# An attention and MLP kernel: the planner's order of operations replaced by a stored table, with other planner settings and full-width products for the first values

## The chip, the cores and the metric

The kernel runs on one core of a Trainium2 chip. A core has a matrix engine (TensorE, PE in the profile, with its weight loads as PEld), a vector engine (VectorE, DVE), a scalar engine (ScalarE, ACT), a general engine (GpSimd, POOL), a queue engine that here only issues DMAs (SyncE, SP), the on-chip memory, and PSUM, eight banks of 128 partitions by 512 float32 that receive the matrix products. Each engine works through its own list of instructions in order, and waits where an instruction needs something that another engine has not finished. The metric is the device time of one execution in microseconds.

## The reference

One input `x` of 2048 rows and 640 columns (bfloat16) goes through two branches, which a gate mixes row by row:

```
g = sigmoid((x * gate_w).sum(-1))
a = softmax(q k^T / sqrt(20)) v, 32 heads of 20 columns, then @ wo       # q, k, v from x @ wqkv
h = x @ w1 + b1 ;  act = h * tanh(softplus(h)) ;  b = act @ w2           # 640 -> 1536 -> 640
out = g * a + (1 - g) * b
```

The attention has 32 heads of 2048 by 2048 scores, all of which pass through an exponential. They are most of the work.

## The kernel before

**Units.** The 32 heads are taken in eight quads `p` of four heads (one head for each 32-row strip of the matrix engine), and the 2048 query columns in four chunks `c` of 512. A pair (p, c) is a group; there are 32 groups of 64 units. A unit is one product of scores: 128 keys of one head by 512 queries, which fills one PSUM bank. Four units that follow one another use the four strips and run beside each other. This is written "S" below: an S operation holds one to four score products.

**Exponentials.** A unit's bank is emptied in one of two ways. ScalarE takes two neighbouring banks (sometimes three or one) through `Exp` into the buffer `E` of 34 slots (line 1122). Or VectorE writes a straight-line approximation of the exponential as 16-bit integers (`psum_chord`, line 1154), and two more versions of it with another offset are made from that copy, each for two units at once, by GpSimd or by VectorE (`line`, line 1172; queue `xq`). A chord unit then enters the next product three times instead of once.

**Values.** The product of `E` with the values is made for four heads at once, in the four 32-column strips ("P", one to four products, into the accumulator bank 7). Two chunks of `VA`, the values with a column of ones, come from `add_v`: j = 0 are the 80 columns of the first four heads, which every unit of the first quad needs.

**The rest of the matrix work** are `Misc` operations: transposes of `x` (`xt`), the projections of queries and keys (`k0`, `q0` for the first quad, blocks `kb`, `qb` for the others), the values (`v0`, `v1`, `v2`), the first and second products of the MLP (`h`, `w2`) and the output projection (`wo`). Each takes a bank, some pieces of matrix work, and one evacuation, mostly by VectorE. Query and key blocks are stored to DRAM and loaded back into strips of the right partitions (`add_blk`, `add_strips`); queries of the first quad's chunks 1 to 3 take this way too, chunk 0 does not.

**Matrix engine modes.** Score products use 32 rows by 128 columns of the array (mode "R"), value products and projections 128 rows by 32 columns, four at a time (`mm4`, mode "C"), transposes the whole array (mode "T").

**What sets the order.** `make_plan` plays the kernel through on the host, with a clock and a duration for every operation. Whenever an engine is free in this play, a function (`poll_pe`, `poll_act`, `poll_dve`, `poll_gp`, `poll_sp`) chooses its next operation from what is ready, by due times and by the numbers in `PAR`, of which those ending in `_2` hold from unit 1700 of 2048 on. What it chooses is appended to `pl.out`, and the kernel is emitted in just that order:

```
    plan = make_plan(K, PAR)
    for fn in plan["pl"].out:
        fn()
```

On the chip only each engine's own order and the data matter; waits are put in wherever an operation touches bytes that an earlier one wrote or read. The settings that the change touches: `v0` moves the due time of the first values (`add_v(0, t, 2 * t - par["v0"])`, due counted in pairs of units, beside `xt` at -100 + 2i, `k0` at -92 + 8c, the first query blocks from -25.6 on); `slack` is how long after the planned end of an exponential its value product may be planned; `elow` is the count of free `E` slots at or under which value products go ahead of projections; `hold` and `idlek` bear on score operations of fewer than three units; `xmin`, `xwait`, `gpmax` and `xb` divide the offset copies between GpSimd and VectorE; `last` keeps the last units from the chord; `wl`, `wp`, `wo` are due times of MLP and output products; `mgb` delays the planned release of a bank.

Of the kernel before, what the change touches and what calls it, by code (L numbers as in the profile page):

```python
# [11 lines left out]
P = 128  # L12
# [8 lines left out]
KT, FT, NS = 5, 12, 16  # L21
# [31 lines left out]
for _c in range(NQC):  # L53
# [8 lines left out]
    "dvw": 38.53743660585776,  # L62
    "gpmax": 3438.021927551807,
    "xmin": 2062.5527122350004,
    "xwait": 349.421302746659,
    "urgent": 22.640125992529832,
    "kq": 2.9970653505716234,
    "v0": 80.0,
    "slack": 154.76747254069397,
    "fill": 0.64,  # L70
    "h0": 3.5649434246577676,
    "h1": 16.826758018508038,
    "w0": 10.794573911905426,
    "w1": 23.39035664805156,
    "hl": 6.335275894690732,
    "wl": 5.8531955315483435,
    "last": 5.05082387060483,
    "mb": 9,
    "elow": 12.382529619172656,
    "ahd": 6.0,  # L80
    "age": 6.220859528764049,
    "eres": 0.014480172002720943,
    "vk": 3,
    "a3": 4,
    "a3gp": 1688.8815596232141,
    "hold": 5,
    "idlek": 5,
    "swait": 155.25662470383708,
    "flush": 8,
    "tailh": 0,  # L90
    "dahead": 387.7453029112783,
    "mgb": 0.0,
    "xb": 0.0,
    "ph": 1700.6915314751984,
    "wp": 30.113523199568974,
    "wo": 26.20880268482808,
    "thr_2": 317.7585558513145,
    "lead_2": 123.43702968058237,
    "gpmax_2": 4098.35985412354,
    "xmin_2": 2880.9153602384567,  # L100
    "xwait_2": 537.2401013960538,
    "vk_2": 3.0,
    "a3gp_2": 1925.808193077294,
    "dahead_2": 447.85548472553995,
    "age_2": 9.211581861796914,
    "ahd_2": 3.0816465538756317,
    "hold_2": 4.0,
    "idlek_2": 3.0,
    "mb_2": 7.0,
    "dvw_2": 36.65964931310165,  # L110
    "slack_2": 253.79751934331,
    "mgb_2": 0.0,
    "xb_2": 1.0,
}

# [5 lines left out]
XAT = [3900.0, 5300.0, 8500.0, 10500.0, 12700.0]  # L121


class Names:
    pass


class Misc:
    def __init__(self, name, due, need, pieces, evac, dur, gives):
        self.name, self.due, self.need = name, due, need  # L130
        self.pieces, self.evac, self.dur, self.gives = pieces, evac, dur, gives
        self.bank = None
        self.i = 0


class Clock:
# [4 lines left out]
    def __init__(self):  # L141
        self.t = 0.0
        self.ev = []
        self.n = 0
        self.free = {e: 0.0 for e in self.LAT}
        self.tok = set()
        self.busy = {e: 0.0 for e in self.LAT}
        self.log = []
        self.out = []
        self.ops, self.cur, self.pend, self.res, self.prov = [], (), [], {}, {}  # L150

    def at(self, t, fn, cur=None):
# [18 lines left out]
    def src(self, toks):  # L171
        return tuple(i for x in toks for i in self.prov.get(x, ()))

    def run(self, eng, occ, done=None, lat=None, rd=(), wr=(), dep=(), kind=""):
        i = len(self.ops)
        deps = set(dep) | set(self.pend)
        self.pend = []
        for r in rd:
            v = self.res.setdefault(r, [None, []])
            deps.add(v[0])  # L180
        for r in wr:
            v = self.res.setdefault(r, [None, []])
            deps.add(v[0])
            deps.update(v[1])
        deps.discard(None)
        for r in rd:
            self.res[r][1].append(i)
        for r in wr:
            self.res[r] = [i, []]
        if lat is None:  # L190
            lat = occ + (36.0 if eng == "GP" else 90.0 if eng in ("DVE", "ACT") else 0.0)
        self.free[eng] = self.t + occ
        self.busy[eng] += occ
        self.log.append((eng, self.t, occ))
        self.ops.append((eng, occ, lat, deps, kind, self.t))
        self.at(self.free[eng], lambda: None)
        if done is not None:
            self.at(self.t + lat + self.LAT[eng], done, (i,))
# [44 lines left out]
def make_plan(K, par):  # L243

    pl = Clock()
# [78 lines left out]
    def bank(b):  # L324
        return K.ps[:, b, :]

    def mm(o, l, r, first, last, pos):
        K.nc.tensor.matmul(o, lhsT=l, rhs=r, start=first, stop=last, tile_position=pos, skip_group_check=True)  # L328

    def mm4(o, l, r, first, last, cols=P):  # L330
        for q in range((cols + 31) // 32):
            w = min(32, cols - 32 * q)
            mm(o[32 * q : 32 * q + w, :], l[:, 32 * q : 32 * q + w], r, first, last, (0, 32 * q))
# [87 lines left out]
    def add_v(j, t0, due):  # L421
        c0, w, h0, nh, nt = VR[j]

        def pc(i, kt, b):
            t = t0 + i
            o = bank(b)[:, i * w : (i + 1) * w]
            mm4(o, K.xT[:, kt, t * P : (t + 1) * P], K.wv[:, kt, c0 : c0 + w], kt == 0, kt == KT - 1)

        def ev(b):
            src = bank(b)[:, 0 : nt * w].rearrange("p (t c) -> p t c", t=nt)  # L430
            o = 1 if j == 1 else 0
            for i in range(nt) if nt != 1 else [0]:
                K.nc.vector.tensor_copy(
                    out=K.VA[:, t0 + i, h0 * VS : (h0 + nh) * VS].rearrange("p (h d) -> p h d", d=VS)[:, :, 0:DH],
                    in_=src[:, i, o : o + nh * DH].rearrange("p (h d) -> p h d", d=DH),
                )
            if j == 1:
                K.nc.vector.tensor_copy(out=K.zt[:, t0 : t0 + nt], in_=src[:, :, 0])

        pieces = []  # L440
        for i in range(nt):
            for kt in range(KT):
                pieces.append((max(w / 2.4, 50.0) + 2.0, "C", (lambda b, i=i, kt=kt: pc(i, kt, b)), ()))
        gives = [("v", j, t0 + i) for i in range(nt)] + ([("z", t0 + i) for i in range(nt)] if j == 1 else [])
        dur = nt * (75 + nh * DH / 0.96) + (70 if j == 1 else 0)
        need = [("xT", t0 + i) for i in range(nt)] + ["wv0" if j == 0 else "wv"]
        misc.append(Misc(f"v{j}.{t0}", due, need, pieces, ev, dur, gives))
# [169 lines left out]
    for c in range(NQC):  # L617
        for f in range(FT):
            k = c * FT + f
# [4 lines left out]
    for t in range(NS):  # L624
        for half in range(2):
            k = 2 * t + half
# [60 lines left out]
    def late_par(k):  # L687
        return par[k + "_2"] if nxt[0] >= par["ph"] else par[k]
# [6 lines left out]
    mode = [None]  # L695
# [5 lines left out]
        return nxt[0] / 2  # L701

    def pe_run(md, dur, done=None, **kw):
        sw = 0.0 if mode[0] == md else 111.0
        mode[0] = md
        recent.append((pl.t + sw, dur))
        pl.run("PE", dur + sw, done, **kw)

    def misc_lim():
        return (NBANK if opn["out"] else NBANK - 2) if opn["tail"] else 3 if opn["lent"] else int(late_par("mb"))  # L710
# [453 lines left out]
    def gp_backlog():  # L1164
        return sum(q[0] for q in gp_q) + 1125.0 * len(xq) + max(0.0, pl.free["GP"] - pl.t)

    xq, lock = [], [0.0]
# [6 lines left out]
    def run_x():  # L1174
        if not xq:
            return False
        idle = pl.free["GP"] <= pl.t and lock[0] <= pl.t and len(xq) >= 2 and not gp_q and late_par("xb") >= 1
        if not idle and (gp_backlog() < late_par("xmin") or lock[0] > pl.t + late_par("xwait")):
            return False
        e0, e, k, w, fin = xq.pop(0)  # L1180
        emit(lambda: line(K.nc.vector, e0, e, k, w))
        wait = max(0.0, lock[0] - pl.t)
        d = 337.0 if w == 2 else 197.0
        lock[0] = pl.t + wait + d - 47.0
        stat["x"] += 1
        pl.run("DVE", wait + d, fin, rd=[("E", e0 + i) for i in range(w)], wr=[("E", e + i) for i in range(w)], kind="X%d" % w)
        return True

    def poll_dve():
# [42 lines left out]
        if run_x():  # L1232
            return True
# [42 lines left out]
        def done():  # L1276
            freed(b)
            push(x, n, h, 0)
            if h == 1:
                third(x, 2)  # L1280
# [16 lines left out]
    def third(x, w):  # L1297
        done = set()

        def fin(k):  # L1300
            done.add(k)
            if len(done) == 2:
                read.add(x[0][0])
                for q in [q for q in held if held[q] == x[0][0]]:
                    del held[q]
                    efree.add(q)
            for n, h in x[2]:
                push(x, n, h, k, len(done) == 2)

        for k in (1, 2):  # L1310
            xq.append((x[0][0], x[0][k], k, w, lambda k=k: fin(k)))

    def flush():
        x, half[0] = half[0], None
# [4 lines left out]
    def poll_gp():  # L1319
        wait = max(0.0, lock[0] - pl.t)  # L1320
        if gp_q:
            dur, fn, done = gp_q.pop(0)
            emit(fn)
            lock[0] = pl.t + wait + dur - 80.0
            pl.run("GP", wait + dur, done, kind="G")
            return True
        if xq:
            e0, e, k, w, fin = xq.pop(0)
            emit(lambda: line(K.nc.gpsimd, e0, e, k, w))
            d = 1125.0 if w == 2 else 650.0  # L1330
            lock[0] = pl.t + wait + d - 82.0
            pl.run("GP", wait + d, fin, rd=[("E", e0 + i) for i in range(w)], wr=[("E", e + i) for i in range(w)], kind="L%d" % w)
            return True
        return False
# [126 lines left out]
def kernel(  # L1461
# [14 lines left out]
    K = Names()  # L1476
# [98 lines left out]
    nc.gpsimd.memset(K.ont, 0.0)  # L1575

    plan = make_plan(K, PAR)
    for fn in plan["pl"].out:
        fn()


# [28 lines left out]
```

## Time and profile before

| | us |
|---|---|
| executions shown | 747.53, 747.78, 748.13 (median 747.78) |
| the profiled execution | 748.59 |
| its span, first to last instruction | 746.7 |

| engine | busy us | share of the span | instructions |
|---|---|---|---|
| PE, matrix products | 731.5 | 98% | 10514 |
| ACT | 715.9 | 96% | 753 |
| DVE | 601.5 | 81% | 1049 |
| POOL | 500.5 | 67% | 466 |

A busy time is the union of an engine's instructions. Matrix products overlap, and their ends are modelled, so that the share of PE says little of how dense the work is: a product of 512 columns is shown 383 ns long, where the next set of four can start after some 217 ns. In the same way an exponential of 1024 columns is shown 1103 ns long, and the next one starts 904 ns after it. Distances from start to start are therefore the better measure for both.

### The profile page before, as it was taken

What the parts mean: (1) busy time and instruction counts of PE and PEld (TensorE: products, weight loads), DVE (VectorE), ACT (ScalarE), POOL (GpSimd) and SP (SyncE); (2) the same over time, 40 slices, a digit from 0 to 9 for tenths busy, and PEclk for the clock granted to TensorE, in tenths of its full rate; (3) what the DMA queues carried; (4) which work ended last, traced back from release to release, by engine and by line L of the source; (5) the groups of instructions that cost most, each with busy time, mean ns of one, the idle gap of its engine ahead of it and who ended that gap; (6) DMA issues with size and microseconds to landing.
All of it is one profiled execution on the core that took longest, in us unless ns stands there. A gap on an engine that the chain in (4) does not pass through costs nothing.

```text
span 746.7 us, 25298 instructions
## 1 busy us (share of the span) xinstructions
PE 731.5 (98%) x10514; PEld 249.9 (33%) x10514; DVE 601.5 (81%) x1049; ACT 715.9 (96%) x753; POOL 500.5 (67%) x466
## 2 busy tenths in 40 slices
PE   8899999999999999999999999999999999999997
PEld 4443322222224433333332222223433333323333
DVE  4478888888888988779888888888998888878785
ACT  6869999999999999999999999999999999999995
POOL 9126666766666767757566755766866678688884
PEclk9999999999999999999999999999999999999999
DMA  9611301020011111112111110003411101212212
GB/s 286 213 61 47 89 17 28 24 61 21 22 28 39 33 30 30 49 41 83 30 44 30 48 45 16 28 22 92 134 48 30 30 25 52 80 51 63 68 38 69
DMA packets 45723, 41.87 MB, mean 56 GB/s; under 512 B 20120, under 2 KB 39240, under 8 KB 45608
## 3 DMA queue, kind: packets, MB, share of 16 engines
q1 hardware_dynamic: 42984, 39.94, 18.0%
q8 instruction: 82, 1.34, 0.8%
q10 hardware_dynamic: 2624, 0.31, 0.3%
q14 instruction: 33, 0.27, 0.1%
HBM read 27.59 MB, written 12.38 MB: 54 GB/s over the span
## 4 chain that ended last, share of the span: by engine, by line
PE 80%; ACT 11%; DVE 4%; issue 3%; DMA 1%; POOL 1%; SPq 0%; POOLq 0%; DVEq 0%; ACTq 0%
PE ps L328 79%; ACT E L1122 11%; DVE E L1154 2%; DVE E L1172 1%; DMA rd_d<-rden 0%; PE ps L1558 0%; POOL E L1172 0%; DMA rb<-rd_d 0%; DVE accs L1213 0%; POOL ost L1031 0%; ACT xT L346 0%; POOL R L1425 0%; PE ps L338 0%; SPq L1411 0%; DVE ost L506 0%
## 5 line engine op out<-in xcount | busy, mean ns | idle before, releaser
L1122 ACT ACTIVATE E<-ps 128x1024 bf16<-128x1024 f32 (+1 forms) x726 | 682.8, 1121 | 19.5 <-PE ps L328 18.6
L1172 POOL TENSOR_SCALAR E<-E 128x1024 uint16<-128x1024 uint16 x396 | 436.6, 1103 | 231.4 <-DVE E L1154 187.0
L1154 DVE TENSOR_SCALAR E<-ps 128x512 uint16<-128x512 f32 x567 | 380.6, 685 | 102.4 <-PE ps L328 92.3
L328 PE MATMUL ps<-qT,kT 32*128 32x512 bf16 x2048 | 287.9, 383 | 4.4 <-ACT E L1122 2.4
L328 PE MATMUL ps<-E,VA 128*32 128x512 bf16 x3182 | 288.8, 383 | 1.1 <-DVE E L1154 0.4
L328 PEld LDWEIGHTS <-kT 32*128 32x128 bf16 x2048 | 78.0, 90 | 271.5 <-issue 266.9
L328 PEld LDWEIGHTS <-VA 128*32 128x32 bf16 x3182 | 72.1, 95 | 93.5 <-issue 81.8
L1172 DVE TENSOR_SCALAR E<-E 128x1024 uint16<-128x1024 uint16 x172 | 95.6, 556 | 7.8 <-DVE E L1154 0.5
L328 PE MATMUL ps<-R,act 128*32 128x320 bf16 x1536 | 84.3, 302 | 0.4 <-DVE E L1154 0.2
L328 PE MATMUL ps<-xT,R 128*32 128x512 bf16 x960 | 79.7, 383 | 0.3 <-ACT E L1122 0.2
L328 PEld LDWEIGHTS <-R 128*32 128x32 bf16 (+1 forms) x1728 | 38.9, 95 | 44.9 <-issue 37.4
L328 PEld LDWEIGHTS <-act 128*32 128x32 bf16 x1536 | 35.5, 95 | 33.9 <-issue 26.1
L328 PE MATMUL ps<-wk,R 128*32 128x320 bf16 (+1 forms) x640 | 39.6, 303 | 0.4 <-ACT E L1122 0.3
L328 PE MATMUL ps<-wv,xT 128*32 128x80 bf16 (+2 forms) x960 | 36.6, 257 | 1.6 <-issue 1.6
L454 DVE TENSOR_SCALAR act<-ps,b1f 128x512 bf16<-128x512 f32 x48 | 35.4, 738 | 1.1 <-PE ps L328 0.7
L328 PE MATMUL ps<-xT,wk 128*32 128x512 bf16 (+1 forms) x360 | 33.2, 383 | 0.0
L1425 POOL TENSOR_TENSOR ons<-accs,rb 128x512 bf16<-128x512 f32 x24 | 31.0, 1293 | 2.6 <-DMA rb<-rd_d 1.1
L328 PE MATMUL ps<-xT,wq 128*32 128x512 bf16 x400 | 32.1, 382 | 0.0
L385 DVE CAST stg<-ps 128x512 bf16<-128x512 f32 (+1 forms) x40 | 27.3, 682 | 2.4 <-PE ps L328 2.3
L328 PEld LDWEIGHTS <-xT 128*32 128x32 bf16 x960 | 19.6, 96 | 15.2 <-issue 10.9
L1213 DVE COPY accs<-ps 128x512 f32<-128x512 f32 x31 | 21.2, 683 | 2.7 <-PE ps L328 2.3
L1046 ACT ACTIVATE act<-act 128x3072 bf16<-128x3072 bf16 x8 | 21.5, 2752 | 0.0
(72 smaller groups left out, 190.1 us busy)
## 6 DMA issues: line engine op xcount, KB each, us to landing
rb<-rd_d SPq DMA_DIRECT2D x124, 64.0 KB
qd<-stg SPq DMA_DIRECT2D x20, 128.0 KB
b_d<-bst SPq DMA_DIRECT2D x16, 160.0 KB
out_dram<-ost SPq DMA_DIRECT2D x16, 160.0 KB
kT<-kd SPq DMA_DIRECT2D x28, 80.0 KB
qT<-qd SPq DMA_DIRECT2D x28, 80.0 KB
stg<-b_d SPq DMA_DIRECT2D x13, 160.0 KB
kd<-stg SPq DMA_DIRECT2D x16, 128.0 KB
```

Of the source, the lines that this page charges most:

```text
L328: K.nc.tensor.matmul(o, lhsT=l, rhs=r, start=first, stop=last, tile_position=pos, skip_group_check=True)
L385: K.nc.vector.tensor_copy(out=K.stg[0:w, s, :], in_=bank(b)[0:w, :])
L454: K.nc.vector.tensor_scalar(out=K.act[:, f, (c % 2) * QC : (c % 2 + 1) * QC], in0=bank(b), scalar1=K.b1f[:, f : f + 1], scalar2=None, op0= ...
L1046: K.nc.scalar.activation(a, a, ACT.Mish)
L1122: lambda: K.nc.scalar.activation(K.E[:, e : e + w, :], K.ps[:, b0 : b0 + w, :], ACT.Exp, scale=SCALE)
L1154: lambda: K.nc.vector.tensor_scalar(out=K.E[:, e + h, :].bitcast(U16), in0=K.ps[:, b, :], scalar1=CH_MUL, scalar2=CH_OFF + CH_ADD[0], op0= ...
L1172: eng.tensor_scalar(out=o, in0=i, scalar1=float(CH_ADD[k]), scalar2=1.0, op0=ALU.add, op1=ALU.mult)
L1213: emit(lambda: K.nc.vector.tensor_copy(out=K.accs[:, g % 2, :], in_=K.ps[:, ACCB, :]))
L1425: gp_q.append((1350.0, lambda: K.nc.gpsimd.tensor_tensor(out=dst(), in0=K.accs[:, b, :], in1=K.rb[:, b, :], op=ALU.mult), lambda: pl.give( ...
```

## The change

- Twenty-two numbers of `PAR` are others, among them `v0` 80 to 64.3, `elow` 12.4 to 20.2, `hold` 5 to 6, `xb` 0 to 1, `slack` 154.8 to 142.0 and `slack_2` 253.8 to 154.4, `gpmax_2` 4098 to 5779, `xmin_2` 2881 to 3533, `mgb_2` 0 to 18.8.
- The pieces of the first values (j = 0) are one product with 128 weight columns each, in mode T, instead of four with 32 in mode C. The host's play counts 62 instead of 50 for such a piece.
- In the host's play, a change of mode costs less where PE has been idle, and GpSimd takes an offset copy at the earliest 90 ns after it was queued.
- Each operation of the plan keeps the emitting functions that belong to it (`fns`), and the kernel emits the operations in the order of a table, `ORDER`, instead of the plan's own. Three hexadecimal digits stand for each operation: its number in the plan, counted from the lowest one not yet emitted. The table has 5,411 entries. Operations that touch the same bytes stay in sequence.

```
-    "slack": 154.76747254069397,
+    "v0": 64.32986463352033,
+    "slack": 141.97275980676932,
...
-    "hold": 5,
-    "idlek": 5,
+    "hold": 6,
+    "idlek": 7,
...
+ORDER = (
+    "01300700500600800900b00000000000000800000000500700000700800a000000000000002000000000000000000000000000000000001000005006001"
...
+)
...
+def unpack(text):
+
+    lo, out = 0, set()
+    for k in range(0, len(text), 3):
+        i = lo + int(text[k : k + 3], 16)
+        yield i
+        out.add(i)
+        while lo in out:
+            out.remove(lo)
+            lo += 1
...
+    def mm1(o, l, r, first, last):
+        mm(o, l, r, first, last, (0, 0))
...
-            mm4(o, K.xT[:, kt, t * P : (t + 1) * P], K.wv[:, kt, c0 : c0 + w], kt == 0, kt == KT - 1)
+            f = mm4 if j else mm1
+            f(o, K.xT[:, kt, t * P : (t + 1) * P], K.wv[:, kt, c0 : c0 + w], kt == 0, kt == KT - 1)
...
-                pieces.append((max(w / 2.4, 50.0) + 2.0, "C", (lambda b, i=i, kt=kt: pc(i, kt, b)), ()))
+                pieces.append((max(w / 2.4, 62.0) + 2.0, "C" if j else "T", (lambda b, i=i, kt=kt: pc(i, kt, b)), ()))
...
-        sw = 0.0 if mode[0] == md else 111.0
+        sw = 0.0 if mode[0] == md else max(0.0, 111.0 - (pl.t - pl.free["PE"]))
...
-        if xq:
-            e0, e, k, w, fin = xq.pop(0)
+        if xq and xq[0][-1] + 90.0 > pl.t + 1e-6:
+            pl.at(xq[0][-1] + 90.0, lambda: None)
+        elif xq:
+            e0, e, k, w, fin, _ = xq.pop(0)
...
-    for fn in plan["pl"].out:
-        fn()
+    for i in unpack(ORDER):
+        for fn in plan["pl"].fns[i]:
+            fn()
```

## The prediction

> **What bounds the kernel now.** I read the page first, then the stages, the waits, and the timeline of the matrix engine.
>
> ```profile
> span 746.7 us, 25298 instructions
> PE 731.5 (98%) x10514; PEld 249.9 (33%) x10514; DVE 601.5 (81%) x1049; ACT 715.9 (96%) x753; POOL 500.5 (67%) x466
> PE 80%; ACT 11%; DVE 4%; issue 3%; DMA 1%; POOL 1%; SPq 0%; POOLq 0%; DVEq 0%; ACTq 0%
> ```
>
> Two engines are nearly full, and the chain that ended last runs mostly along PE. The stages tell where either one rests:
>
> ```profile
> 20.00:30.00 10.00, 9.78 (x221) 4.52 (x219) 4.08 (x11) 10.00 (x13) 0.95 (x2) 1.00 0.97 337
> 30.00:40.00 10.00, 8.27 (x202) 3.38 (x198) 6.29 (x18) 6.85 (x8) 2.99 (x3) 1.00 0.08 26
> 40.00:60.00 20.00, 20.00 (x357) 8.90 (x354) 15.01 (x32) 12.81 (x14) 5.02 (x5) 1.00 0.22 67
> 400.00:450.00 50.00, 49.88 (x623) 13.96 (x627) 43.05 (x71) 50.00 (x55) 32.87 (x30) 1.00 0.15 39
> 650.00:700.00 50.00, 48.01 (x643) 15.73 (x639) 38.37 (x64) 49.47 (x54) 40.70 (x39) 1.00 0.22 66
> 740.00:747.00 7.00, 2.55 (x76) 1.76 (x68) 3.30 (x7) 1.58 (x3) 2.55 (x3) 0.96 0.27 96
> ```
>
> The columns are the stage, its length, then PE, PEld, DVE, ACT and POOL busy, the clock (1.00 nearly throughout), and DMA. ACT loses 3.15 + 7.19 = 10.3 us between 30 and 60 us, and almost nothing from there to 730. Measured from start to start, where a 1024-column exponential takes 904 ns and a 1536-column one 1331, ACT's spacings exceed these by 18 us in all between 50 and 725 us: about 8.6 us in 20 gaps over 250 ns, the rest in small ones.
>
> ```profile
> ACT E L1122 <- PE ps L328: 18.6, 20, 7.1
> PE ps L328 <- ACT E L1122: 2.8, 11, 0.5
> POOL E L1172 <- DVE E L1154: 187.0, 158, 11.1
> PE ps L328 <- issue: 1.6, 2, 1.4
> ```
>
> (Waiter, releaser: us in total, times, longest.) ACT waits for scores; PE hardly waits for anybody. So in the body PE's own work is the limit:
>
> ```profile
> 104.19 0.62 PE L328 MATMUL ps<-E,VA 128*32 128x512 bf16 x8
> 104.74 0.39 PE L328 MATMUL ps<-qT,kT 32*128 32x512 bf16 x3
> 105.06 0.62 PE L328 MATMUL ps<-xT,R 128*32 128x512 bf16 x8
> 105.61 0.39 PE L328 MATMUL ps<-qT,kT 32*128 32x512 bf16 x3
> ```
>
> Start to start, a run of scores takes 320 ns whether it holds two, three or four products: 217 ns and about 103 for the change of mode; the eight value products take 550 = 2 x 217 and a change. Counted over the whole timeline of PE there are 721 runs of scores and 739 others. Runs of scores work 157 us, C-mode products 375, transposes 6, 1459 changes at 103 ns are 150: 688 of PE's 738 us; 50 are left, some 13 of them rounds of one to three value products, which cost as much as four. PE and ACT are thus balanced within a few per cent, and a faster ACT alone, or a faster PE alone, would soon meet the other.
>
> **The change part by part.** The sum is made against the profiled execution: 748.59 us, of which 746.7 are span and 1.9 lie around it. It is 0.8 above the median 747.78.
>
> *Settings without effect.* `a3` is only tested for truth; `idlek` is compared with at most four units, so 5 and 7 both mean never. The 90 ns rule is no instruction; POOL rests 187 us waiting for chord copies, so its cost is 0, and if that cover were gone, 394 x 0.09 = 35 us of POOL.
>
> *First values.* 320 products become 80. The row:
>
> ```profile
> L328 PE MATMUL ps<-wv,xT 128*32 128x80 bf16 x320 | 5.9, 202 | 1.6 <-issue 1.6
> 33.39 0.87 PE L328 MATMUL ps<-wv,xT 128*32 128x80 bf16 x76
> 10.64 1.36 PE L338 MATMUL ps<-ident,act 128*128 128x128 bf16 x18
> 11.93 0.39 PE L328 MATMUL ps<-qT,kT 32*128 32x512 bf16 x2
> ```
>
> 19 sets of four take from 33.39 to 34.36, less a change: 46 ns a set. The nearest row for 128 weight columns are transposes: 18 from 10.64 to 11.93, less a change, 66 ns each. So 80 x 20 = +1.6 us of PE, if a transpose's price holds; the lower end is 80 x (80/128 x 66 - 46) = -0.4 if the price goes with the columns streamed. Against it, the only two issue waits of PE fall on these products, 1.6 us. With a quarter of the instructions they may go; 0 to -1.6. What follows an issue wait, scores for ACT, is then earlier by as much. I take +1.6 - 1.6 = 0, range -2.0 to +1.6. A change of mode more or less is 0.1 us each; scores stand between the runs anyway.
>
> The Trainium skill (TensorE: Matmul & The Clock Gate, Back-to-back issue gap) gives some 81 ns for each pair of weight load and 128-column product; this trace's transposes show 66. By the page the first values would cost 80 x 35 = 2.8 us more instead of 1.6, an estimate from its figure. Its section on weight loads has 128 columns take 107 ns, which the 66 contradict.
>
> *The start.* ACT works from 10.74 us and has the 64th unit of the first group at 40. The next group needs the strip of its queries: block projected from 35.11 to 39.3, stored at 40.55, strips issued from 42.38, first scores at 47.70. Meanwhile ACT rests 7.1 us. With `v0` 64.3 the first values come after all transposes and all `k0`, still before the query block. So value products cannot start before about 25 us (now 20.38): the eight rounds of them that PE runs between 20 and 30 us are put off, 8 x 217 = 1.7 us, and projections move forward by that. The store and the eight strip loads on SP follow the block and move with it; SP issues nothing between 22.7 and 40.55, so nothing is queued before them. Cost of the delay: 34 slots of `E` are 17 exponentials, 10.74 + 17 x 0.904 = 26.1 us, where ACT must stop until value products free slots. The transposes of five tiles and two `k0` pushed ahead of the first values are 25 x 66 ns + 10 x 217 ns = 3.8 us, in gaps of some 0.5 us in each 0.9 us round: 7 us later than 15.34, and the first values land near 25.5. That is just in time. I take -2 us; the ends are -7.1 (rest gone) and +3 (values two rounds late and one more chunk after them).
>
> *The body.* The table and the settings change how scores, value products and chords interleave. 94% of the 5,411 entries stand within ten places of the plan's order, so it is local work. A planner run of the old settings has 5,389 operations; 22 more can be five chord pairs more (one exponential less, four operations more each; ACT -0.9 us, PE +0.2 us) or more partial rounds (PE +0.2 to 0.4 us each): no sign follows. What can be won without fewer operations is ACT's 18 us at most; each run of scores saved gives PE 0.42 us. I take half of the 8.6 us in long gaps: -4.3. The ends are -13 (the long gaps and half of the small ones) and +5 (the rival below).
>
> *The end.* After the last exponential (736.3) 10.4 us remain, mostly one after the other through DMA, POOL and the last products; `last` keeps one unit more from the chord. 0, range -2 to +1.
>
> Sum: 0 - 2 - 4.3 + 0 = -6.3: 748.6 becomes 742.3, or 741.5 against the median.
>
> **The rivals.** *It changes nothing:* the gaps that the search closes exist only in the play on the host, and new small ones open. For it: PE waits 2.8 us for exponentials in the whole span, so the order already fits the chip. 747.8 within 1.5.
>
> *Slower: value products wait at the head of PE.* An order fixed with less slack (`slack_2` 154 instead of 254) puts value products close behind the copies they read. PE is in order: a waiting value product holds the scores behind it, and ACT with them. Which copies are late can be read: an offset copy on DVE takes 332 ns at its shortest and 556 in the mean, POOL's of 1125 ns start up to 1177 apart, as if each sometimes waited for the other. If a quarter of the 566 offset copies exposed the 224 ns by which DVE's differ from their shortest, PE would lose 32 us; against it, today's order exposes almost none (1.0 us on chord copies). It decides against the change where about 5% of them, 28 x 0.224 = 6.3 us, come to be exposed. I price it at 8%: 45 x 0.224 = 10 us, so 751.5.
>
> The Trainium skill (SBUF — State Buffer, Who interferes with whom) states that DVE in a two-port mode and GpSimd lock each other out for a whole instruction; the 556 against 332 ns agree. By it lateness comes in whole instructions, up to POOL's 1.1 us.
>
> *More:* the rest at 40 us goes (-7.1), and the 8.6 us of long gaps: 748.6 - 15.7 = 732.9, 732 against the median. For it: both are plain in any play on the host. Against it: the block is still due after the first values.
>
> **How the numbers follow.** Forecast (736 to 746.2) 0.45, more 0.18, no change 0.14, slower 0.23. A difference under 0.2%, 1.5 us, can't be told from none here. So faster 0.63, same 0.14, slower 0.23. The range reaches the third case and the priced slower one with a little more: 731 to 753; the likeliest case alone, 736 to 746.
>
> **What would show it.** First values: 80 products of 128 by 128 with 80 columns and no issue wait near them; the distance in a run of them tells 66 ns from 46. Start: scores of the second group before 46 us, ACT's loss between 30 and 60 us under 9 us. Body: fewer runs of scores than 721, or fewer exponentials of ACT with its spacings as now; ACT's excess between 50 and 725 us under 14 us. The slower rival would show as PE waits on ACT, DVE or POOL well above 5 us. It would be wrong above all if the number of exponentials or of runs moved by more than ten, which I can't see from here, or if the first values came late enough to stop ACT at 26 us.

## The result: 1.2% slower, and the profile after

| executions | before, same chip | after |
|---|---|---|
| shown | 747.53 to 750.01 (four) | 756.54 to 757.81 (four) |
| median | 747.95 | 757.66 |
| profiled execution | 748.59 | 757.71 |

The ratio is 1.0121 (95% interval 1.0100 to 1.0142): 9.1 us slower, beyond the upper end of the predicted range. First the totals of the kernel after, with its chain that ended last by engine:

```profile
span 755.8 us, 24862 instructions
PE 736.3 (97%) x10282; PEld 256.9 (34%) x10282; DVE 613.2 (81%) x1074; ACT 717.7 (95%) x754; POOL 483.9 (64%) x453
PE 77%; DVE 9%; ACT 8%; issue 4%; DMA 1%; POOL 1%; SPq 0%; POOLq 0%; DVEq 0%; ACTq 0%
```

The work is about the same. PE has 232 products fewer (240 fewer first values), ACT one instruction more, POOL makes 13 offset copies fewer and DVE 19 more; the span is 9.1 us longer all the same. So the time is in how the work is strung together. The stages of the kernel after (stage, length, then PE, PEld, DVE, ACT and POOL busy, clock, DMA):

```profile
0.00:10.00 10.00, 6.02 (x52) 3.30 (x56) 1.71 (x6) 3.74 (x6) 9.33 (x21) 1.00 0.85 280
...
30.00:40.00 10.00, 9.30 (x144) 4.69 (x146) 7.44 (x22) 8.89 (x10) 4.88 (x5) 1.00 0.05 17
40.00:60.00 20.00, 19.88 (x372) 9.33 (x364) 14.21 (x29) 12.26 (x14) 7.95 (x8) 1.00 0.21 62
400.00:450.00 50.00, 49.63 (x618) 13.65 (x610) 41.03 (x69) 49.49 (x55) 33.80 (x31) 1.00 0.15 43
550.00:600.00 50.00, 49.23 (x703) 16.37 (x700) 44.46 (x72) 47.65 (x52) 30.32 (x27) 1.00 0.12 32
650.00:700.00 50.00, 47.52 (x694) 17.29 (x692) 43.38 (x75) 49.40 (x53) 34.27 (x32) 1.00 0.25 71
```

ACT still rests before the second group: 1.11 + 7.74 = 8.9 us between 30 and 60 us, against 10.3. From 550 to 600 it rests 2.35 us, where in the kernel before it was busy for 49.08 of the 50:

```profile
550.00:600.00 50.00, 49.80 (x741) 16.26 (x744) 43.07 (x76) 49.08 (x54) 34.80 (x31) 1.00 0.10 28
```

The waits of the kernel after (waiter, releaser: us, times, longest):

```profile
ACT E L1274 <- PE ps L476: 15.7, 24, 6.0
...
ACT E L1274 <- issue: 6.7, 2, 6.2
...
PE ps L476 <- DVE E L1306: 3.3, 8, 0.9
PE ps L476 <- ACT E L1274: 3.2, 12, 0.5
PE ps L489 <- ACT xT L497: 2.1, 1, 2.1
```

ACT's two long waits here lie in the first 50 us: 6.0 us before its first exponential, and 6.2 before the second group, put down to "issue" because the profile shows no releaser. (In the kernel before the rest ahead of the second group is the 7.1 us among its waits for PE.) No wait of the body stands out; PE waits some 2 us more on DVE's and 0.4 more on ACT's handling of `E`. The new item is the last: a single wait of PE for ACT at the very start.

The most useful view was worked out from the timeline of PE: when the first score product of each group of 64 units starts, in us. (e1 to e12 are the experiments below.)

| group | before | after | e1 | e12 | e5 | e3 |
|---|---|---|---|---|---|---|
| 0 | 10.3 | 14.5 | 10.4 | 10.2 | 10.2 | 10.2 |
| 1 | 47.7 | 49.4 | 46.8 | 45.1 | 45.1 | 45.9 |
| 6 | 156.5 | 158.9 | 156.1 | 155.3 | 154.3 | 155.1 |
| 19 | 447.6 | 449.4 | 444.5 | 443.6 | 444.8 | 446.1 |
| 26 | 606.7 | 614.1 | 609.0 | 607.6 | 610.0 | 605.2 |
| last unit | 733.6 | 742.8 | 736.7 | 735.8 | 738.7 | 732.1 |

The kernel after loses 4.2 us before its first scores, has won 2.5 of them back at group 1, is at +1.8 at group 19, and loses 5.6 more by group 26.

### The profile page after: what moved, and what is told of

It reads as the page before. It is cut to its first block, busy times and chain, and to the rows that moved or that the text cites. A ratio compares the mean times of both kernels' runs of the same rounds, so it can differ in the third digit from the quotient of the medians.

```text
span 755.8 us, 24862 instructions
## 1 busy us (share of the span) xinstructions
PE 736.3 (97%) x10282; PEld 256.9 (34%) x10282; DVE 613.2 (81%) x1074; ACT 717.7 (95%) x754; POOL 483.9 (64%) x453
## 4 chain that ended last, share of the span: by engine, by line
PE 77%; DVE 9%; ACT 8%; issue 4%; DMA 1%; POOL 1%; SPq 0%; POOLq 0%; DVEq 0%; ACTq 0%
PE ps L476 77%; ACT E L1274 7%; DVE E L1306 5%; DVE E L1324 2%; DMA wq<-in_A_wqkv_dram 1%; DMA qT<-qd 0%; DVE act L606 0%; DVE stg L536 0%; POOL E L1324 0%; POOL ost L1183 0%; PE ps L489 0%; SPq L546 0%; POOL R L1579 0%; DVE VA L585 0%; SPq L429 0%
## 5 line engine op out<-in xcount | busy, mean ns | idle before, releaser
L1274 ACT ACTIVATE E<-ps 128x1024 bf16<-128x1024 f32 (+2 forms) x727 | 684.5, 1099 | 24.6 <-PE ps L476 15.7
L1324 POOL TENSOR_SCALAR E<-E 128x1024 uint16<-128x1024 uint16 x383 | 419.3, 1095 | 255.5 <-DVE E L1306 208.4
L476 PE MATMUL ps<-E,VA 128*32 128x512 bf16 x3194 | 300.9, 383 | 1.6 <-DVE E L1324 0.8
L1324 DVE TENSOR_SCALAR E<-E 128x1024 uint16<-128x1024 uint16 x191 | 108.5, 568 | 6.7
L476 PEld LDWEIGHTS <-VA 128*32 128x32 bf16 x3194 | 78.5, 95 | 99.8 <-issue 83.5
L476 PE MATMUL ps<-R,act 128*32 128x320 bf16 x1536 | 87.0, 302 | 0.0
L476 PE MATMUL ps<-xT,R 128*32 128x512 bf16 x960 | 84.5, 383 | 0.2 <-DVE E L1306 0.2
L476 PE MATMUL ps<-wv,xT 128*32 128x241 bf16 (+2 forms) x720 | 37.1, 276 | 0.7 <-DVE E L1306 0.3
L476 PEld LDWEIGHTS <-xT 128*32 128x32 bf16 (+1 forms) x720 | 19.4, 96 | 13.6 <-issue 10.8
```

Source lines behind the costliest of these rows:

```text
L1274: lambda: K.nc.scalar.activation(K.E[:, e : e + w, :], K.ps[:, b0 : b0 + w, :], ACT.Exp, scale=SCALE)
L1324: eng.tensor_scalar(out=o, in0=i, scalar1=float(CH_ADD[k]), scalar2=1.0, op0=ALU.add, op1=ALU.mult)
```

## The experiments

Each ran beside the kernel before on the same chip; a ratio is to that, with its 95% interval. Parts are given in us as differences of ratios times 748.

**e1: the plan's order without the table; e2: first values in four strips; e3: only the full-width first values.**

```
e1 (after)                              e2 (after)
-    for i in unpack(ORDER):            -    f = mm4 if j else mm1
-        for fn in plan["pl"].fns[i]:   +    f = mm4
-            fn()
+    for fn in plan["pl"].out:          e3 (before)
+        fn()                           -    mm4(o, K.xT[...], K.wv[...], ...)
                                        +    f = mm4 if j else mm1
                                        +    f(o, K.xT[...], K.wv[...], ...)   # mm1 as in the change
```

> The changed kernel with all its settings and its full-width first values, but emitted in its plan's own order instead of the table's. If the table's order makes the loss (theory T), the time falls back to 746 to 750 us and the scores of the group numbered 26 start within 2 us of the 606.7 us of before. If the new settings and the altered play make it (theory S), the time stays at 755 to 759 us. If only the order of ScalarE's first four operations in the table matters (theory A), 755.5 to 756.5: the first exponential is back near 10.8 us, and the 1.7 us by which the second group is late go, while the other 7 stay.

> The changed kernel with the first values in four products of 32 columns again; settings and table as changed. If the full-width products cost what a transpose costs (66 instead of 46 ns, 80 times), up to 1.6 us faster: 756 to 757. If they are paid back by the issue waits that go, the same within 0.5 us. If they were a main cause of the loss, below 754.

> The kernel before with nothing but the first values as one product of 128 columns; plan and order untouched. By the prediction's first term, 0 within -2.0 to +1.6 us of the kernel before; the issue wait of 1.4 us near 30 us is gone. If the form of these products is the cause of the loss, over 2 us slower.

Measured: e1 752.45, 1.0045 (1.0030 to 1.0060); e2 758.24, 1.0127 (1.0110 to 1.0144); e3 747.16, 0.9984 (0.9971 to 0.9997). The first values in full width gain 1.2 us by themselves (e3). In the table's order the same edit can't be told from nothing (e2 against after). The settings and the changed rules of the play cost 4.6 us (e1 against e3), and what the table adds is another 5.7: e1 lies between the times of its two theories, and each had half of the loss.

The row of the first values in e3, and its timeline there (start, length):

```profile
L328 PE MATMUL ps<-wv,xT 128*128 128x80 bf16 x80 | 5.3, 202 | 0.0
...
31.97 0.87 PE L328 MATMUL ps<-wv,xT 128*128 128x80 bf16 x19
32.83 0.40 PE L328 MATMUL ps<-qT,kT 32*128 32x512 bf16 x4
```

The issue wait of 1.6 us is gone, and 19 products take 0.86 us, less a change 0.76: 40 ns each, where a set of four narrow ones took 46. Both averages hold the end of their run; from start to start the full-width products and the narrow sets are alike, 36 ns apart (medians). By the table e3 is 1.8 us early at group 1 and 1.4 to 1.5 early at all later groups. A small gain at the start thus lasts, under the same later order, to the end.

**e4 and e5: one copy on ScalarE elsewhere.** In the table, the copy of the first query weights (`wqp`, operation 19) is ACT's first instruction. The start of ACT's timeline, after:

```profile
5.79 0.54 ACT L446 ACTIVATE wqp<-wq 128x400 bf16<-128x400 bf16 x1 [2.48 <-DMA wq<-in_A_wqkv_dram]
6.23 0.52 ACT L446 ACTIVATE wkp<-wk 128x400 bf16<-128x400 bf16 x1
6.65 0.68 ACT L497 ACTIVATE xT<-ps 128x640 bf16<-128x640 bf16 x1
```

and before:

```profile
4.51 0.54 ACT L298 ACTIVATE wkp<-wk 128x400 bf16<-128x400 bf16 x1 [1.21 <-DMA wk<-in_A_wqkv_dram]
5.25 0.70 ACT L346 ACTIVATE xT<-ps 128x640 bf16<-128x640 bf16 x1 [0.21 <-PE ps L338]
5.86 0.53 ACT L298 ACTIVATE wqp<-wq 128x400 bf16<-128x400 bf16 x1
```

The query weights land late. Put first, their copy holds the evacuation of the first transposes, 6.65 instead of 5.25, and that bank is what PE waits for. PE after:

```profile
4.02 1.25 PE L489 MATMUL ps<-ident,act 128*128 128x128 bf16 x10
7.39 1.22 PE L489 MATMUL ps<-ident,act 128*128 128x128 bf16 x10 [2.12 <-ACT xT L497]
9.20 2.32 PE L476 MATMUL ps<-xT,wkp 128*32 128x512 bf16 x20 [0.58 <-DVE xT L499]
11.30 2.35 PE L476 MATMUL ps<-xT,wqp 128*32 128x512 bf16 x20
```

and PE before:

```profile
3.97 1.25 PE L338 MATMUL ps<-ident,act 128*128 128x128 bf16 x10
5.41 0.90 PE L338 MATMUL ps<-ident,act 128*128 128x128 bf16 x10 [0.19 <-DMA act<-in_A_x_dram]
7.10 1.26 PE L328 MATMUL ps<-xT,wkp 128*32 128x512 bf16 x20 [0.79 <-ACT xT L346]
8.18 1.27 PE L328 MATMUL ps<-xT,wqp 128*32 128x512 bf16 x20
```

The late start is 2.0 us; on top, the same 20 products take 2.10 us from start to start (9.20 to 11.30) instead of 1.08, and the next 20 take 2.28 instead of 1.20. So about half of the 4.2 us by which the first scores are late is waiting, and half is PE at half its rate. PE is so slow at the start of both kernels (the ten transposes at 4 us take 1.25 us in each, ten of them at 9.38 us in the kernel before 0.73), but the kernel before is at full rate from 5.8 us on, the kernel after only from 13.7. The last section comes back to this.

```
e4, e5 (after)
-    for i in unpack(ORDER):
+    order = list(unpack(ORDER))
+    order.remove(19)
+    order.insert(order.index(12) + 1, 19)     # e4: behind the first transposes' evacuation
+    order.insert(order.index(25) + 1, 19)     # e5: behind the second's instead
+    for i in order:
```

> The changed kernel with the table, in which one operation is moved: the copy of the first query weights on ScalarE stands behind the first evacuation of a transpose again, as before, instead of first of all. Theory A: the first exponential comes near 10.8 us instead of 14.96, the second group's scores start 1.5 to 2 us earlier, and the whole is 1 to 2 us faster, 755.5 to 756.7. If the body absorbs the start, less than 0.5 us. If the late start were all of the loss, 748 to 750.

> The changed kernel with its table, but ScalarE's copy of the first query weights stands behind both of its transpose evacuations, so that the arrival of these weights holds neither. If the place of this one copy is the table's main loss (theory A, made larger by the first runs), 752 to 754 us in all executions, first exponential near 10.8 us. If the table's other moves lose as well, 755 to 757. The difference to the plan's own order under the same settings (752.45) is what the rest of the table is worth: under 0 the moves gain, over 0 they lose.

Measured: e4 755.45, from 753.22 to 759.10, 1.0092 (1.0055 to 1.0129); e5 753.30, 1.0066 (1.0052 to 1.0080). e5 gives 4.1 us back. ACT and PE in e5:

```profile
4.76 0.69 ACT L497 ACTIVATE xT<-ps 128x640 bf16<-128x640 bf16 x1
...
6.82 0.53 ACT L446 ACTIVATE wqp<-wq 128x400 bf16<-128x400 bf16 x1
```

```profile
6.99 1.26 PE L476 MATMUL ps<-xT,wkp 128*32 128x512 bf16 x20 [0.58 <-DVE xT L499]
8.08 1.25 PE L476 MATMUL ps<-xT,wqp 128*32 128x512 bf16 x20
```

The 20 products take 1.09 us again. e4 is inconclusive as an average: two of its four executions took 4 to 6 us more than the other two. The slowest is the one that was profiled, and shows why:

```profile
10.03 0.54 ACT L446 ACTIVATE wqp<-wq 128x400 bf16<-128x400 bf16 x1 [4.49 <-DMA wq<-in_A_wqkv_dram]
```

There the weights landed at 10 us, and whatever stands behind their copy waits. Its stages of 5 to 15 us show PE resting and then slow (the clock column is the one with 0.75 and 0.56):

```profile
5.00:10.00 5.00, 0.72 (x10) 0.73 (x11) 0.77 (x2) 0.54 (x1) 5.00 (x8) 0.75 1.02 378
10.00:15.00 5.00, 3.79 (x40) 1.50 (x39) 0.69 (x1) 1.13 (x2) 5.00 (x7) 0.56 1.09 321
```

e5's place, behind both evacuations, is the safer.

**e8: the same copy put first in the kernel before.**

```
e8 (before; the plan's operations keep their functions, as in the change)
+    order = list(range(len(plan["pl"].fns)))
+    order.remove(19)
+    order.insert(0, 19)
```

> The kernel before with one operation moved: ScalarE's copy of the first query weights stands first, as in the table. Theory A: first scores 4 us later (14.3 instead of 10.3) and 2 to 4.5 us slower in all. If the later first group takes the delay up (it waits for its queries near 40 us anyway), under 1 us.

Measured: 750.47, 1.0027 (1.0014 to 1.0041), 2.0 us. Its first scores start at 13.5, 3.2 us late, and its second group 1.7 us late, and 1.7 us late it stays to the end. What is caught up in between is not taken from ACT's rest before the second group, which is 7.12 us as in the kernel before. PE's wait on issue among the narrow first values is shorter by 1.4 us (1.6 in the kernel before):

```profile
PE ps L331 <- issue: 0.2, 1, 0.2
```

The kernel after and e5 have no such wait, and there nothing is caught up: against e5 the kernel after is 4.3 us late at its first scores and 4.3 at its second group.

**e6, e7, e10, e11: single settings in the kernel before.** Is a changed setting worth something by its meaning, or is every plan a new draw?

```
e6:  -    "slack": 154.76747254069397,     +    "slack": 156.3,
e7:  -    "xwait": 349.421302746659,       +    "xwait": 352.9,
e10: -    "slack": 154.76747254069397,     +    "slack": 141.97275980676932,
e11: -    "wl": 5.8531955315483435,        +    "wl": 6.4206626210236575,
```

> The kernel before with one setting moved by 1% (slack 154.8 to 156.3), which means nothing by itself but makes the play choose otherwise from some point on. If the settings' loss is that of any new draw of the plan (theory D), 750 to 754 us, 2 to 6 slower than before. If the loss comes from what the new settings mean (theory S), within 1 us of the kernel before.

> A second draw: the kernel before with xwait moved by 1% (349.4 to 352.9). Theory D: 750 to 754 us, by another amount than the first draw. Theory S: within 1 us of the kernel before.

> The kernel before with one setting as in the change (slack 142.0 instead of 154.8). Its plan has 37 value rounds of fewer than four products in groups 19 to 26; the kernel before has 20, the changed one 32. Theory D (a different draw of the plan loses what the old draw had there): groups 19 to 26 take 3 to 5 us more than the 159.2 us of before, and the whole is 751 to 755 us. Theory S (what some other setting means, such as wl or elow): within 1.5 us of before.

> The kernel before with the due times of the second MLP product spread as in the change (wl 6.42 instead of 5.85). Its plan has 44 rounds of fewer than four value products in groups 19 to 26. Theory D: groups 19 to 26 take 4 to 6 us more than before, the whole 751 to 756 us, and more than with the slack alone. If only this setting's meaning counts, the same here and no loss with the slack alone.

Measured: e6 748.69, 1.0008 (0.9995 to 1.0021); e7 748.24, 0.9995 (0.9984 to 1.0006); e10 759.26, 1.0135 (1.0118 to 1.0153); e11 757.04, 1.0105 (1.0086 to 1.0125). e6 and e7 turned out to test nothing: e7's plan is the plan of before, and e6's differs by two pairs of operations that changed places. They do show that the same order gives the same time. e10 and e11 each make one of the change's edits alone, and each alone loses more than all of them together (e1, 4.6 us more than e3), and more than was expected of it. So the numbers' effects don't add up. The play on the host tells part of this: it ends at 736.1 us for the kernel before, 748.4 for e10, 745.2 for e11 and 737.4 for the plan of e1. The losses of e10 and e11 (10.1 and 7.9 us) stand in the play already; the loss of e1 mostly doesn't.

Where three of these plans lose is the same stretch: from group 19 to 26 the kernel before and e3 take 159.1 us, e1 164.5, e10 164.3, e11 163.8. In e1's timeline 59 sets of value products there are partial (fewer than four products), in the kernel before 26, and with all counted e1 has 211 sets instead of 188: 23 x 217 ns = 5.0 us, the size of the loss in these groups. The timelines of e10 and e11 hold 201 and 206 sets there, 43 and 61 of them partial: 2.8 and 3.9 us of their 5.2 and 4.7. From group 1 to the last unit e1 has only 13 sets more than the kernel before (857 and 844), 2.8 of its 4.0 us. No run takes only the partial sets away, so this is an account that fits in part, not a proof. The windows of 440 to 520 us, e10 and then before:

```profile
440.00:520.00 80.00, 78.08 (x1162) 28.69 (x1157) 63.45 (x103) 74.46 (x78) 49.46 (x46) 1.00 0.21 57
```

```profile
440.00:520.00 80.00, 79.83 (x984) 22.67 (x980) 66.02 (x111) 79.60 (x86) 52.21 (x47) 1.00 0.15 41
```

ACT runs 78 instructions instead of 86 and rests 5.5 us, while PE issues 178 products more, among them 272 of the MLP's second product, of which the kernel before has none there: a setting changes by a few per cent, and whole pieces of other work land in a stretch where PE has no room for them.

**e12: only the start of the table; e9: its long runs of scores undone.** Both have the copy where e5 has it.

```
e12 (e5's order)                            e9 (e5's order)
+    order[876:] = sorted(order[876:])      +    for r in runs:   # 18 stretches of the list, 572 entries,
                                            +        order[r[0] : r[-1] + 1] = sorted(order[r[0] : r[-1] + 1])
```

(In e9 the stretches reach twelve entries to either side of every place where two score operations that follow one another on PE hold five units or more; sorted is the plan's own order.)

> The changed kernel's plan in its own order except for the first 876 operations (to about 112 us), which stand as in the table, with the query weights' copy last. The table's start gains 1.4 us on the plan's order by the fourth group (110.0 instead of 111.4 us); if its moves after that are what loses, 750.5 to 751.5 us, under both the plan's own order (752.45) and the table (753.3). If the table loses nothing after 112 us, 753.

> The table with the query weights' copy last (753.3 us), in which 18 stretches of some 25 to 60 entries go back to the plan's order: those around places where two score operations stand together so that a run of five or more scores results (23 places, of which one stays). Theory M: such a run saves two changes of mode (0.21 us) but its last scores wait for a bank that ScalarE has not emptied (0.3 us and more each, 5.9 us in 25 runs by the trace), and ScalarE then starves; undone, the waits before scores fall from 11.1 towards 7 us and the time to 750 to 752 us. If the runs of five and more only replace changes of mode by equal waits, 753 within 0.7 us.

Measured: e12 750.36, 1.0024 (1.0010 to 1.0037); e9 755.43, 1.0086 (1.0071 to 1.0102). Up to 112 us (e12) the table gains 1.6 us over the plan's own order (e1); what it does from there on costs 3.1 us (e5 against e12). My theory for these 3 us was that the table joins runs of scores into runs of five to seven units, which then wait for banks. e9 leaves 3 such runs of 25 and is 1.5 us slower than e5, outside both of its forecasts. Four of its 18 stretches lie before 112 us, so that it also gives up 1.1 us of the table's start (155.4 at group 6 against 154.3); from there to the last unit it takes 584.8 us, e5 584.4 and e12 580.5. Undoing the long runs wins nothing back, so the theory fell.

What the table's body does show in an account of PE between group 1 and the last one (sets at 217, 135 or 102 ns for 512, 320 and 241 columns, plus 103 ns a change of mode; the rest is waiting and partial sets):

| | mode changes | work us | rest us | time us |
|---|---|---|---|---|
| before | 1388 | 644.1 | 41.8 | 685.9 |
| e1 | 1397 | 645.8 | 44.4 | 689.9 |
| e12 | 1393 | 645.6 | 45.3 | 690.5 |
| e5 | 1349 | 640.9 | 52.8 | 693.6 |
| after | 1349 | 640.9 | 52.5 | 693.3 |

From e12 to e5 the table saves what can be counted, 44 changes of mode, 4.7 us of PE, and it comes with 7.5 us more of rest. Most of that stands before scores. Taken from start to start, beyond these prices and from 50 us on, what is lost before score products is 8.2 us in the kernel before, 7.8 in e1, 8.3 in e12 and 13.0 in e5; before value products it is 2.6, 3.5, 3.7 and 4.2. The rows of the score products from 50 us on, e12 and then e5 (idle time of PE before them, and what ended it), show the same way:

```profile
L476 PE MATMUL ps<-qT,kT 32*128 32x512 bf16 x1972 | 275.3, 384 | 4.1 <-ACT E L1274 2.5 <-DVE E L1306 0.4 <-DVE stg L536 0.2
```

```profile
L476 PE MATMUL ps<-qT,kT 32*128 32x512 bf16 x1969 | 275.6, 383 | 5.6 <-ACT E L1274 2.3 <-DVE E L1306 1.4 <-DVE R L699 0.3
```

**e13 and e14: the table for PE alone, and for the other engines alone.** The table moves 1723 of 2975 places on PE, 408 of 1037 on DVE, 146 of 418 on POOL, 18 of 745 on ACT. In e13 PE has the table's order and the others the plan's (DVE but for 39 places, which the data force); in e14 the other way round (PE but for 67 places).

```
e13, e14 (after, `wqp` copy as in e5)
-ORDER = ( ...the table... )
+ORDER = ( ...the same operations, one side in the order of the table, the other in the plan's... )
```

> The changed plan with the table's order on the matrix engine alone; the other engines work in the plan's own order (VectorE but for 39 of 1037 places), the query weights' copy behind both transposes. Theory P (the table's places on the matrix engine lose after 112 us, by score runs that wait for banks or value rounds that wait for copies): 753 to 755 us, as the whole table (753.3) or worse, with waits before scores near 11 us. Theory V (the places on VectorE and GpSimd lose): 750 to 751, as with the table's start alone (750.36).

> The mirror: the plan's order on the matrix engine (but for 67 of 2975 places), the table's on VectorE, GpSimd and ScalarE, the query weights' copy behind both transposes. Theory P: 752 to 753 us, as the plan's own order, with no gain at the start. Theory V: 754 to 756. If the two halves lose together only what neither loses alone, both kernels are at 751 to 752.5.

Measured: e13 773.87, 1.0332 (1.0313 to 1.0351); e14 776.49, 1.0364 (1.0344 to 1.0384). Neither side carries the 3 us: mixed, they lose 20 and 22 us against e5, and more against e1. Both are far above every time that was named for them beforehand. Waits of e13, then e14, then e5:

```profile
ACT E L1274 <- PE ps L476: 27.1, 33, 5.6
PE ps L476 <- DVE E L1306: 12.9, 20, 1.5
```

```profile
ACT E L1274 <- PE ps L476: 29.6, 53, 3.3
PE ps L476 <- DVE E L1306: 10.5, 20, 1.1
```

```profile
ACT E L1274 <- PE ps L476: 12.9, 24, 3.3
PE ps L476 <- DVE E L1306: 3.5, 9, 0.9
```

ACT's wait for scores more than doubles, and PE waits on DVE at least three times as long: the orders of the engines hold only together.

**e15: the parts that gained.** The kernel before, with the full-width first values and the copy of the query weights behind both evacuations.

```
e15 (before)
-    mm4(o, K.xT[...], K.wv[...], ...)
+    f = mm4 if j else mm1
+    f(o, K.xT[...], K.wv[...], ...)
...
+    order = list(range(len(plan["pl"].fns)))
+    order.remove(19)
+    order.insert(order.index(25) + 1, 19)
```

> The kernel before with the two things that the runs show to be right: the first values as full-width products, and the copy of the first query weights behind both transposes on ScalarE. 746.5 to 747.5 us, at or just under the full-width products alone (747.2), and fewer late executions.

Measured: 747.25, 0.9975 (0.9958 to 0.9992), faster than both kernels by 0.25% and 1.4%. Against e3 (0.9984) the moved copy can't be told from nothing: in the profiled execution of the kernel before it was not waited for. It can be, in that order too: in e6's profiled execution (752.38 us), where this copy stands as in the kernel before, the weights landed at 8.7 us, and the first scores started at 15.4. Fewer late executions were expected of e15 and are not shown: two of its twelve took 751.3 us, four of the seventeen of the kernel before beside it over 750.5.

## Why the prediction was wrong, step by step

The parts, as the runs divide the 9.1 us. They are steps from the kernel before over e3, e1, e12 and e5 to the kernel after, so they sum to the whole by construction; from another start a part can have another size, as the copy costs 4.1 us here and 2.0 in the kernel before (e8). By the intervals each is good to 1 to 1.5 us.

| part | from | us |
|---|---|---|
| full-width first values | e3 against before | -1.2 |
| settings and rules of the play | e1 against e3 | +4.6 |
| table to 112 us (copy as in e5) | e12 against e1 | -1.6 |
| table from 112 us on | e5 against e12 | +3.1 |
| place of the `wqp` copy on ACT | after against e5 | +4.1 |

**Settings without effect (0): half right.** `a3` and `idlek` alone leave the plan as it was, and so do eleven more of the twenty-two numbers. But the 90 ns rule is no instruction and still not free: it alone gives another plan, as do the other two rule changes and nine settings. I asked what it costs on POOL, when the question was what it does to the order.

**First values (0, range -2.0 to +1.6): a term mis-sized, within its range.** From start to start a full-width product costs 36 ns, not the 66 of a transpose, and a narrow set costs 36 as well, not 46. The 66 held waits inside the run: the transposes start 56 ns apart (median). Their weight loads are shown 106 ns long in the mean and overlap, so the 66 did not contradict a load of 107. The issue wait went as hoped. No change for the products and -1.6 for the wait make -1.6, of which e3 measured 1.2.

The row is 36 ns from one pair of weight load and product to the next. The Trainium skill (TensorE: Matmul & The Clock Gate, Back-to-back issue gap) gives about 81 ns for such pairs with 128 columns streamed, and for a product alone columns / 2.4 GHz + 2.5 ns, an estimate of 36 ns for 80 columns. The measurement is the second, and the first did not bind here.

**The start (-2, ends -7.1 to +3): failed.** The measure is e3, which has the full-width products but neither the new `v0` nor the table, and whose second group comes at 45.9. With the settings it comes at 46.8 (e1), with the table's start and without the late copy at 45.1 (e12, e5): +0.9 and -0.8 us instead of -2. The value products do start late, at 24.93 in e1, but the projections did not move forward by it: the query block is projected from 35.79 on, in e3 from 33.30, in the kernel before from 35.11. And the slots were not "just in time": ACT rests 1.6 us at 25.4 in e1. In the kernel after the second group comes at 49.4, because I priced the settings and not the table's first entries, though these say in which order ACT runs its first three instructions, and the timeline of before shows `wqp` harmless at 5.86, behind the evacuation. The 4.1 us of this copy, half of them from PE at half rate, were in no term of the sum and in no rival.

**The body (-4.3, ends -13 to +5): the step that failed most.** It measured about +6.8, outside its range: the settings' +4.6, of which some 0.9 fall before the second group, and the table's +3.1 from 112 us on. I wrote "no sign follows" from a plan with another number of operations, and then gave it a sign all the same, half of the long gaps. The plan of before was not an average one: e10, e11 and e1 each lose against it. Nor did the work that the table saved turn into time: the table's 4.7 us of PE came with 7.5 us of new rest, most of it before score products.

**What would show it.** First values: right (80 products, no issue wait; the 36 ns lie below both of the prices named). Second group before 46 us: no, 49.4. ACT's loss between 30 and 60 us under 9 us: yes, 8.9, and nothing won by it. Fewer runs of scores than 721: yes, 696, and no faster, so this sign was a bad one. ACT's excess between 50 and 725 us under 14 us: no, it rose from 18.2 to 24.7.

**The rivals.** "Changes nothing" was wrong for the sum, though its reason held: what the play closes, the chip opens elsewhere. The slower rival had the right sign and a size too small, 751.5, and not the mechanism. Its price was mis-read, too: 332 ns is a distance from start to start and 556 a duration; by duration the shortest of these copies takes 412 ns, which leaves 144 to be exposed instead of 224. Its sign, "PE waits on ACT, DVE or POOL well above 5 us", came in part: at `E` 3.3 us on DVE and 3.2 on ACT, 6.5 against 3.8 in the kernel before, and 2.1 at the start. But what grows with the table's body is the time lost before score products, from 8.3 us in e12 to 13.0 in e5; before value products, where this rival puts it, it goes from 3.7 to 4.2.

**Left open:** which waits make the table's 3 us from 112 us on. The loss grows slowly (e5 against e12: -1.0 us at group 6, +1.2 at 19, +2.4 at 26, +2.9 at the last unit), it shows as PE standing before score products, with 1.0 us more of it put down to DVE, but no row carries all of it, and undoing the long runs won nothing back.

## What to carry to other kernels

An order found on a model is fitted to the model: judge a new table or a new set of planner numbers as a new draw, measured on the chip, and not by the gaps that it closes in the play; with PE and ACT both within a few per cent of full, other draws of the same planner were 5 to 10 us slower. Ask the play for its own end all the same: it had the losses of e10 and e11 in advance, though not those of e1. When an order is stored, read its first entries against the landing times of the loads: one copy of 0.5 us put ahead of its DMA on an in-order engine cost 4 us here and 2 in the kernel before. Fewer mode changes or fewer runs are no gain by themselves, if the engine then stands for as long. The longer rest was measured; what makes it is open.

## What the hardware showed that was not expected

- PE at half rate while the profile's clock column reads 1.00. PE starts at half rate in every profiled execution (the first sets of 512 columns start 0.42 us apart, later ones 0.217), and the column reads 1.00 there because the trace's clock record is empty until full speed begins: at 5.81 us in the kernel before, at 13.72 in the kernel after, where the products change their pace at the same moment (ten transposes from 13.58 on start 79, 90 and then 56 ns apart). A late copy is not needed for it. In e11 the weights landed as in the kernel before and PE's rests are the same (0.18 and 0.79 us, 0.19 and 0.79 there), and yet full speed began at 10.46 and the first scores came 1.8 us late:

```profile
5.39 1.25 PE L338 MATMUL ps<-ident,act 128*128 128x128 bf16 x10 [0.18 <-DMA act<-in_A_x_dram]
7.44 2.33 PE L328 MATMUL ps<-xT,wkp 128*32 128x512 bf16 x20 [0.79 <-ACT xT L346]
```

  Where PE then rested longer, full speed ended again 3.41 us after it had begun, and came back 6.83 and 6.82 us later (e4: 4.12, 7.53, 14.36; e6: 5.58, 8.99, 15.81). The Trainium skill (TensorE: Matmul & The Clock Gate, Part 1) says that the array falls to half its clock after an idle window of about 3.4 us, and is back after as long a busy one; the 3.41 us and the factor of two agree. That the rests of the kernel after fell into two such windows, and so kept PE slow until 13.7, fits these figures; no run tests it.
- The landing of the query weights varies: 5.8 us in the profiled execution of the kernel after, 8.7 in e6's and 10.0 in e4's, with the order of the loads the same.
- Full-width first values (a 128-column weight load, 80 columns streamed) start 36 ns apart, just as sets of four narrow products do, with a quarter of the instructions. The wait on issue stood only among the narrow products: 0 to 1.6 us in the seven profiled executions that have them, none in the ten others.
